# Gate and val products of a gated feed-forward block in seven half-size products instead of eight

## The chip, the cores and the metric

One core of a Trainium2 chip runs the whole program: TensorE (PE) multiplies, VectorE (DVE), ScalarE (ACT) and GpSimd (POOL) do the elementwise work, and transfers are issued on the queue of SyncE (SP). The metric is the device time of one execution in microseconds, as the median of three runs.

## The reference, cut to what matters

Attention over 4 batches of 8 heads gives x with 2304 tokens of 512 features. Two feed-forward blocks follow; the change is in the second, in which gate and val are two products of the same x.

```python
def _moe_ref(x, w_in, w_out, s, b):          # d_ff = 2048
    r = np.maximum(x @ w_in, 0.0)
    return ((s * (r * r) + b) @ w_out)

def _moe2_ref(x, w_gate, w_val, w_out):      # d_ff = 1536
    g = x @ w_gate
    silu = g * (1.0 / (1.0 + np.exp(-g)))
    val = x @ w_val
    return (silu * val @ w_out)
```

The weights arrive as 64-bit floats, the activations as 32-bit ones.

## The kernel before, in words

Every operand of a product is split into a high and a low part (fp32r), and a product is three matmuls: high by high, high by low, low by high (`mm3`). The program has three stages: attention, the first block (`block_b`, five blocks of 512, 512, 512, 384 and 384 tokens) and the second block (`block_2`, the same five blocks of tokens).

In `block_b` a chunk is 128 of the 2048 hidden features. PE makes `hb` (12 matmuls), ACT and DVE make the square and its two parts (`relu`, `sq`, `gh`, `gl`), and PE adds the chunk before it into `acc` (12 matmuls). The normalised x of a block is prepared by `x_load`: a sum of two loads and a product with `rbx`, on POOL, then the split on ACT and DVE.

In `block_2` before the change, for each of the 12 chunks `f`, gate and val take four steps over the 512 features each, three matmuls a step, as wide as the block of tokens (512 or 384 columns). ACT makes silu, DVE multiplies, both split the result, and `second` multiplies it with `out2` (matmuls of 512 columns, 3 for each 128 tokens). All 36 weights stay on chip once they are split.

A weight comes by `weight`: a load of 512 KB into `raw` (3 buffers), four steps that turn it into 32 bits (`d0` on ACT, `d1` to `d3` on DVE, in one of 2 `dec` buffers), then its high part on ACT and its low part on DVE or POOL, in one of 36 weight slots (pools `wa` 10, `wb` 22, `wc` 4), of which the first block's weights take 32.

The order of the instructions is set at build time by `Schedule`: it keeps a clock with assumed durations, and on each engine issues the ready operation of lowest `prio` whose buffers are free. On the chip every engine then works through its own list strictly in that order, and an instruction that waits holds up everything behind it on its engine.

Of the kernel before, what the change touches and what calls it, by code (L numbers as in the profile page):

```python
# [177 lines left out]
def tile_attention_moe_moe(  # L178
# [79 lines left out]
    y_d = [dram.tile([DM, n], F32, name=f"y_d{j}") for j, n in enumerate(UBS)]  # L258
# [13 lines left out]
    W, W_op, W_tok = {}, {}, {}  # L272

    def weight(key, pools, prio, dep=None, hi_eng="act", lo_eng="pool", after=()):
# [7 lines left out]
        raw_tok, slot_tok = Token("raw"), Token(*pools)  # L282
# [11 lines left out]
        o = sch.dma(n * 262144, load, prio, (dep,), (raw_tok,), after=after, pace=1.5)  # L294
# [28 lines left out]
        else:  # L323
            end = (raw_tok,)

        def hi():
            p = wa_p if slot_tok.pool == "wa" else late[slot_tok.pool]
            W[key] = p.tile([128, 2, 512], F32R, tag="w", name="w")
            val = st["val"] if wide else st["raw"]
            if hi_eng == "act":  # L330
                nc.scalar.activation(out=W[key][:, 0], in_=val, func=AF.Copy)  # L331
            else:
                nc.vector.tensor_copy(W[key][:, 0], val)

        def lo():
            val = st["val"] if wide else st["raw"]
            e = nc.gpsimd if lo_eng == "pool" else nc.vector
            e.tensor_tensor(out=W[key][:, 1], in0=val, in1=W[key][:, 0].bitcast(F32), op=ALU.subtract)  # L338
# [400 lines left out]
    def x_load(st, pieces, n, prio, deps, pool_name, pool, batches=None):  # L739

        xh_tok = Token(*pool_name)
# [175 lines left out]
    def block_b(i, j):  # L917
# [8 lines left out]
        outs, xh_tok = x_load(st, pieces, UB, prio - 800 if i else LATE - 900, deps, ("xhb", "xhc"), lambda: late[st["xh_tok"].pool], batches)  # L926
# [12 lines left out]
        for d in range(KD):  # L939
# [5 lines left out]
            y_op[j].append(sch.dma(512 * UB, lambda d=d, st=st, j=j: nc.sync.dma_start(out=y_d[j][d * 128:(d + 1) * 128, :], in_=st["y", d]),  # L945
# [5 lines left out]
    z = 0  # L951
    for f in range(F2):
        for kind in ("gate", "val", "out2"):
            weight((kind, f), ("wb", "wa", "wc"), LATE + 2500 + 120 * z, sw, lo_eng="pool" if z % 2 else "dve")
            z += 1

    def block_2(i, j):
        st = {}
        UB = UBS[j]
        prio = LAST + 2000 * i  # L960
        outs, xh_tok = x_load(st, [(0, UB, (y_d[j],))], UB, prio - 1500 if i else LATE + 1000 * n_b, y_op[j], ("xhb", "xhc"), lambda: late[st["xh_tok"].pool])
        nt = UB // 128
        a_toks = (Token("s"), Token("s"))
        acc_toks = (a_toks[0], a_toks[0], a_toks[1], a_toks[1])
        step = 0
        pend = None
        hs, order = chains["gb"]

        def second(pend, first, last):
            f, gops, g_tok = pend  # L970
            res = []
            for c in range(nt):
                def fn(c=c):
                    if first and c == 0:
                        st["acc"] = []
                        for _ in range(2):
                            t = ps_s.tile([128, 1024], F32, tag="s", name="acc2")
                            st["acc"] += [t[:, 0:512], t[:, 512:1024]]
                    w = W["out2", f]
                    uh, ul = st["u", f]  # L980
                    cs = slice(c * 128, (c + 1) * 128)
                    o = st["acc"][c]
                    nc.tensor.matmul(o, uh[:, cs], w[:, 0], start=first, stop=False)  # L983
                    nc.tensor.matmul(o, uh[:, cs], w[:, 1], start=False, stop=False)  # L984
                    nc.tensor.matmul(o, ul[:, cs], w[:, 0], start=False, stop=last)  # L985
                res.append(op("pe", t_mm(512, 3), fn, prio + step, (*gops, W_op["out2", f], *order[-1:]), a_toks if first and c == 0 else (),
                              (g_tok, W_tok["out2", f])))
                order.append(res[-1])
            return res

        for f in range(F2):
            toks = {}
            last_mm = {}
            for kind in ("gate", "val"):
                tok = toks[kind] = Token("t", "v")
                for kk in range(KD):
                    def fn(kk=kk, f=f, kind=kind, tok=tok):
                        if kk == 0:
                            st[kind, f] = get_hb(tok, UB)
                        w = W[kind, f]  # L1000
                        cs = slice(kk * 128, (kk + 1) * 128)
                        mm3(st[kind, f], w[:, 0, cs], w[:, 1, cs], st["xh"][:, kk], st["xl"][:, kk], kk == 0, kk == KD - 1)
                    hs.append(op("pe", t_mm(UB, 3), fn, prio + step, (outs[kk], W_op[kind, f], *hs[-1:]), (tok,) if kk == 0 else (),
                                 (xh_tok, W_tok[kind, f])))
                    step += 1
                last_mm[kind] = hs[-1]
            r_tok, g_tok = Token("rb2"), Token("gb")
            def silu(f=f):
                st["u", f] = tuple(late["gb"].tile([128, 512], F32R, tag=tag, name=tag)[:, 0:UB] for tag in ("gh", "gl"))
                st["si", f] = late["rb2"].tile([128, 512], F32, tag="r", name="si")[:, 0:UB]  # L1010
                nc.scalar.activation(out=st["si", f], in_=st["gate", f], func=AF.Silu)  # L1011
            def mul(f=f):
                nc.vector.tensor_tensor(out=st["si", f], in0=st["val", f], in1=st["si", f], op=ALU.mult)  # L1013
            def uh(f=f):
                nc.scalar.activation(out=st["u", f][0], in_=st["si", f], func=AF.Copy)  # L1015
            def ul(f=f):
                nc.vector.tensor_tensor(out=st["u", f][1], in0=st["si", f], in1=st["u", f][0].bitcast(F32), op=ALU.subtract)
            o = op("act", t_act(UB), silu, prio + step, (last_mm["gate"],), (r_tok, g_tok), (toks["gate"],))
            o = op("dve", t_dve(UB), mul, prio + step, (o, last_mm["val"]), (), (toks["val"],))
            o1 = op("act", t_act(UB, False), uh, prio + step, (o,))  # L1020
            o2 = op("dve", t_dve(UB), ul, prio + step, (o1,), (), (r_tok,), port=True)
            if pend is not None:
                second(pend, pend[0] == 0, False)
                step += nt
            pend = (f, (o1, o2), g_tok)
        fin = second(pend, False, True)
        for c in range(nt):
            y_tok = Token("rb2")
            def ev(y_tok=y_tok, c=c):
                st["y", c] = late["rb2"].tile([128, 512], F32, tag="r", name="o")  # L1030
                if c % 2:
                    nc.vector.tensor_copy(st["y", c], st["acc"][c])
                else:
                    nc.scalar.activation(out=st["y", c], in_=st["acc"][c], func=AF.Copy)
            o = op("dve" if c % 2 else "act", 0.6, ev, prio + 1900, (fin[c],), (y_tok,), (acc_toks[c],))
            for z in range(2):
                b, g = divmod((sum(UBS[:j]) + c * 128) // 64 + z, PC)
                last = i == len(blocks) - 1 and z == 1
                def put(c=c, z=z, b=b, g=g, e=nc.scalar if last else nc.sync):
                    e.dma_start(out=out[b * S:(b + 1) * S].rearrange("(r g) m -> r g m", g=PC)[:, g], in_=st["y", c][64 * z:64 * z + 64])  # L1040
                sch.dma(131072, put, prio + 1900, (o,), (), (y_tok,), eng="act" if last else "sp")

    for i, j in enumerate(blocks):
        block_2(i, j)
# [45 lines left out]
```

## Time and profile before

| what | value |
|---|---|
| median of 3 runs | 1173.27 us (1172.63 to 1173.53) |
| the profiled execution | 1175.48 us, its span 1173.7 us |
| PE busy | 1143.1 us (97%), 6242 matmuls |
| PE weight loads busy | 1009.1 us (86%) |
| DVE busy | 616.2 us (52%) |
| ACT busy | 551.5 us (47%) |
| POOL busy | 263.6 us (22%) |
| moved by DMA | 110.39 MB, mean 94 GB/s |

Busy is the time that an engine spent on instructions; a matmul's end is modelled and overlaps the next one's start, so how fast matmuls follow each other is read from their starts. In the timeline, times are from the span's start.

### The profile page before, as it was taken

Reading aid. Unit: us, or ns where it says so; the run is one execution under the profiler, and the core shown is the slowest. Engines: PE = TensorE matmul, PEld = TensorE weight load, DVE = VectorE, ACT = ScalarE, POOL = GpSimd, SP = SyncE. Lnnn points to the kernel's source line nnn. Section 1 sums busy time; section 2 is a strip of 40 time slices with the busy share of each in tenths; the row PEclk is TensorE's granted clock in tenths of the full one; section 3 lists DMA queues with packets and bytes.
Section 4 is the critical chain, followed back from the end, with each engine's and each line's share of the span. In section 5 each row is a group of like instructions: output and inputs, shape, how many; then the busy total and the mean of one; then the engine's idle time right before and its main releaser. Section 6 shows DMA issues by size and latency. Waiting matters only on the chain.

```text
span 1173.7 us, 16604 instructions
## 1 busy us (share of the span) xinstructions
PE 1143.1 (97%) x6242; PEld 1009.1 (86%) x6242; DVE 616.2 (52%) x969; ACT 551.5 (47%) x1112; POOL 263.6 (22%) x222
## 2 busy tenths in 40 slices
PE   8989899999999999999999999999999999999998
PEld 7889888898887888888899998888888888899997
DVE  5879788999979943232242798811211211211111
ACT  4879888899877832232232566412111211211211
POOL 6776685743222031020020112200000000000000
PEclk8899999999999999999999999999999999999999
DMA  4588888767375640110110446301100200200100
GB/s 112 117 191 189 228 208 190 201 158 183 94 226 177 216 149 17 56 57 5 64 49 6 135 146 218 112 1 47 25 1 1 63 1 1 63 1 1 27 1 27
DMA packets 126335, 110.39 MB, mean 94 GB/s; under 512 B 68256, under 2 KB 103216, under 8 KB 126256
## 3 DMA queue, kind: packets, MB, share of 16 engines
q1 hardware_dynamic: 126016, 108.95, 34.3%
q8 instruction: 49, 0.80, 0.3%
q10 hardware_dynamic: 240, 0.39, 0.1%
q14 instruction: 30, 0.25, 0.1%
HBM read 69.71 MB, written 18.95 MB: 76 GB/s over the span
## 4 chain that ended last, share of the span: by engine, by line
PE 79%; DVE 8%; ACT 4%; DMA 3%; SPq 2%; issue 2%; POOL 1%; ACTq 0%; POOLq 0%; DVEq 0%
PE hb L798 14%; PE hb L800 14%; PE hb L799 14%; PE acc L799 5%; PE acc L800 5%; PE acc L798 5%; PE acc L983 4%; PE acc L985 4%; PE acc L984 4%; PE ps_s L609 3%; PE ps_t L670 2%; DVE nm L612 2%; SPq L537 2%; DVE pl L685 2%; PE ps_av L700 1%
## 5 line engine op out<-in xcount | busy, mean ns | idle before, releaser
L798 PE MATMUL hb<-xh,w 128*128 128x512 f32 (+1 forms) x800 | 296.3, 370 | 1.9 <-ACT w L331 1.4
L800 PE MATMUL hb<-xh,w 128*128 128x512 f32 (+1 forms) x800 | 296.0, 370 | 0.0
L799 PE MATMUL hb<-xl,w 128*128 128x512 f32 (+1 forms) x800 | 295.6, 370 | 0.0
L1013 DVE TENSOR_TENSOR si<-hb,si 128x512 f32<-128x512 f32 (+1 forms) x60 | 38.3, 638 | 276.4 <-PE hb L800 273.3
L798 PEld LDWEIGHTS hb<-xh,w 128*128 128x128 f32 x800 | 150.2, 188 | 23.8 <-ACT w L331 1.8
L800 PEld LDWEIGHTS hb<-xh,w 128*128 128x128 f32 x800 | 150.1, 188 | 21.0 <-DVE w L338 0.4
L799 PEld LDWEIGHTS hb<-xl,w 128*128 128x128 f32 x800 | 150.1, 188 | 21.0
L799 PE MATMUL acc<-gl,w 128*128 128x512 f32 (+1 forms) x320 | 118.2, 369 | 0.1
L1011 ACT ACTIVATE si<-hb 128x512 f32<-128x512 f32 (+1 forms) x60 | 33.3, 555 | 180.0 <-PE hb L800 174.3
L798 PE MATMUL acc<-gh,w 128*128 128x512 f32 (+1 forms) x320 | 117.9, 368 | 0.0
L800 PE MATMUL acc<-gh,w 128*128 128x512 f32 (+1 forms) x320 | 117.7, 368 | 0.0
L612 DVE TENSOR_REDUCE nm<-ps_s 128x1 f32<-128x576 f32 x144 | 108.3, 752 | 11.7 <-PE ps_s L609 10.4
L609 PE MATMUL ps_s<-t,a 128*128 128x288 f32 x320 | 103.6, 339 | 9.1 <-ACT e L616 7.4
L616 ACT ACTIVATE e<-ps_s,nm 128x576 f32<-128x576 f32 x144 | 107.1, 744 | 8.3 <-DVE nm L612 7.5
L678 ACT ACTIVATE ph<-ps_t 128x512 fp32r<-128x512 f32 x192 | 105.8, 570 | 9.6 <-PE ps_t L670 7.8
L1015 ACT ACTIVATE gh<-si 128x512 fp32r<-128x512 f32 (+1 forms) x60 | 35.4, 589 | 146.2 <-DVE si L1013 146.2
L850 DVE SCALAR_TENSOR_TENSOR r<-r,sv 128x512 f32<-128x512 f32 (+1 forms) x64 | 46.2, 722 | 108.0 <-ACT r L844 108.0
L700 PE MATMUL ps_av<-ph,vh 128*128 128x384 f32 (+1 forms) x320 | 97.8, 326 | 0.4 <-ACT xr L713 0.4
L844 ACT ACTIVATE r<-hb 128x512 f32<-128x512 f32 (+1 forms) x80 | 44.0, 551 | 114.9 <-PE hb L800 103.6
L685 DVE TENSOR_TENSOR pl<-ps_t,ph 128x512 fp32r<-128x512 f32 x144 | 96.0, 684 | 1.8 <-ACT ph L678 0.6
L670 PE MATMUL ps_t<-ident,e 128*128 128x128 f32 x576 | 88.4, 281 | 6.9 <-DVE qklo L515 4.3
L609 PE MATMUL ps_s<-kz,a 128*128 128x288 f32 x320 | 92.8, 305 | 0.1
(80 smaller groups left out, 1962.4 us busy)
## 6 DMA issues: line engine op xcount, KB each, us to landing
raw<-in_moe_w_out_dram SPq DMA_DIRECT2D x28, 512.0 KB, 3.6
x_d<-xr SPq DMA_DIRECT2D x64, 144.0 KB, 2.6
raw<-in_moe_w_in_dram SPq DMA_DIRECT2D x16, 512.0 KB, 3.9
raw<-in_moe_w_gate_dram SPq DMA_DIRECT2D x12, 512.0 KB, 3.5
raw<-in_moe_w_val_dram SPq DMA_DIRECT2D x12, 512.0 KB, 3.7
x<-in_q_dram SPq DMA_DIRECT2D x15, 288.0 KB, 3.6
x<-in_k_dram SPq DMA_DIRECT2D x15, 288.0 KB, 5.0
out_dram<-o SPq DMA_DIRECT2D x33, 128.0 KB, 2.4
```

Source lines behind the costliest of these rows:

```text
L609: nc.tensor.matmul(ps[:, hf * 512:hf * 512 + HS], a[:, q0:q0 + 128], m[:, k0:k0 + HS], start=y == 0, stop=y == len(todo) - 1)
L612: nc.vector.tensor_reduce(out=st["nm"][:, u:u + 1], in_=st["s", u], axis=AX.XY, op=ALU.max, negate=True)
L616: nc.scalar.activation(out=st["e", u].rearrange("p (f n) -> p f n", f=2), in_=st["s", u], func=AF.Exp, bias=st["nm"][:, u:u + 1], accum_ou ...
L670: nc.tensor.transpose(ps[:, z * 128:z * 128 + 128], st["e", u][:, kc * 128:kc * 128 + 128], ident)
L678: nc.scalar.activation(out=st["ph", y][0:rows, 512 * i:512 * i + n], in_=st["pt", y, i][0:rows, 0:n], func=AF.Copy)
L685: nc.vector.tensor_tensor(out=dst, in0=st["pt", y, i][0:rows, 0:n], in1=st["ph", y][0:rows, c].bitcast(F32), op=ALU.subtract)
L700: nc.tensor.matmul(ps, vv, st["ph", y][:, c], start=kc == 0, stop=kc == 4)
L798: nc.tensor.matmul(o, lh, rh, start=first, stop=False)
L799: nc.tensor.matmul(o, lh, rl, start=False, stop=False)
L800: nc.tensor.matmul(o, ll, rh, start=False, stop=last)
L983: nc.tensor.matmul(o, uh[:, cs], w[:, 0], start=first, stop=False)
L984: nc.tensor.matmul(o, uh[:, cs], w[:, 1], start=False, stop=False)
```

## The change

Gate and val of one chunk are now made for 768 tokens at a time (three blocks instead of five). The 512 features are halved, the 768 tokens are halved (`QN` = 384), and gate and val are the two halves of the third direction. By Strassen's scheme (in Winograd's form) seven products of 256 features by 384 tokens, each of 6 matmuls of 384 columns, take the place of eight.

- **Sums of weights.** `combine` loads and decodes gate and val of a chunk, makes four sums on DVE, splits the results into four pairs of parts and stores them (`keep`) in DRAM (`wd`), with the split `out2` as the fifth. This is done four chunks at a time during blocks 1 to 3 of `block_b`. Slots are given back when the store has landed.
- **Sums of x.** `x_load_2` loads four quarters of a block's x and makes four differences (768 columns, DVE) and seven splits (ACT and DVE).
- **A chunk.** `unit` makes the seven products; of their results ACT copies one and DVE adds seven times (384 columns), in buffers of `rb2`, `raw` and `dec`. The first 384 tokens go on to `out2` (`out_proj` with h=0) one chunk later, between the products. For the second 384 tokens the result is kept in six weight slots; after the twelfth chunk these are split and multiplied in one run (`out_proj` with h=1, 12 times 9 matmuls).
- **Stream.** For every block the four parts of each chunk are loaded again from `wd` into weight slots; the 12 parts of `out2` are loaded once and stay.
- In `x_load` the sum and the product with `rbx` of blocks 1 to 4 move from POOL to DVE, and POOL's low parts of weights go to DVE.

```diff
-    y_d = [dram.tile([DM, n], F32, name=f"y_d{j}") for j, n in enumerate(UBS)]
+    y_d = dram.tile([DM, NT], F32, name="y_d")
+    wd = [[dram.tile([2, 128, 512], F32, name=f"wd{f}_{z}") for z in range(5)] for f in range(F2)]
...
+    def keep(f, z, prio, after, dep, n, tok, tile):
+        def put():
+            nc.sync.dma_start(out=wd[f][z].rearrange("h p m -> p h m")[:, :, 0:n], in_=tile()[:, :, 0:n].bitcast(F32))
+        wd_op[f, z] = sch.dma(1024 * n, put, prio, (dep,), (), (tok,), after=after, pace=1.2)
...
+        gst, g_o, g_end = fetch(("gate", f), prio, None, after, (s_tok,))
+        vst, v_o, v_end = fetch(("val", f), prio + 1, None, (W_ld["gate", f],))
...
+        for fn in (s1, s2, s3, s4):
+            o = (op("dve", t_dve(HALF), fn, prio + 2, o, port=True),)
...
+        weight(("out2", f), ALL, prio + 10, None, lo_eng="dve", after=(W_ld["val", f],))
+        keep(f, 4, prio + 10, (), W_op["out2", f], 512, W_tok["out2", f], lambda f=f: W["out2", f])
...
-        for kind in ("gate", "val", "out2"):
-            weight((kind, f), ("wb", "wa", "wc"), LATE + 2500 + 120 * z, sw, lo_eng="pool" if z % 2 else "dve")
+        gate = chains["gb"][0][KD * (F1 * (1 + f // 4) + 3 * (f % 4) + 1)]
+        ld_last = (combine(f, LATE + 1000 * (1 + f // 4) + 700 + 20 * (f % 4), (*ld_last, gate)),)
...
+    PRODS = ((0, 0), (0, 1), (1, 0), (2, 0), (3, 0), (1, 1), (2, 1))
+    X_OF = ("b11", "b21", "t2", "t3", "t4", "t1", "b22")
...
+                    for kk in range(2):
+                        mm3(ps[z], wh, wl, xh, xl, kk == 0, kk == 1)
...
+            for z, when in enumerate((0, 1, 2, 3, 4, 11, 13)):
+                product(z, when)
```

Three places show how the order changes. Names: `r` and `gl` belong to a chunk of the first block, `dec` to decoding, `sums` and `w` to the new sums of weights, `xsum`, `xl`, `xh` to the sums of x.

DVE in block 3 of `block_b`, before:

```order
L850 SCALAR_TENSOR_TENSOR r<-r,sv 128x384 [waits Activation_49]
L862 SCALAR_TENSOR_TENSOR gl<-r,bv,gh 128x384 [waits Activation_49]
L787 TENSOR_TENSOR xl<-xs,xh 128x384 [waits DMAHW2_49,DMAHW1_49,Activation_49]
L850 SCALAR_TENSOR_TENSOR r<-r,sv 128x384 [waits DMAHW5_49,DMAHW0_49,Activation_49]
L862 SCALAR_TENSOR_TENSOR gl<-r,bv,gh 128x384 [waits PE_49,Activation_49]
```

The same engine and block now:

```order
L310 SCALAR_TENSOR_TENSOR dec<-raw,dec 128x512 [waits DMAHW6_49,DVE_49]
L315 SCALAR_TENSOR_TENSOR dec<-raw,dec 128x512 [waits DVE_49]
L874 SCALAR_TENSOR_TENSOR gl<-r,bv,gh 128x384 [waits PE_49,Activation_49]
L993 TENSOR_TENSOR sums<-dec 128x256 [waits DVE_49]
L996 TENSOR_TENSOR sums<-sums,dec 128x256 [waits DVE_49]
L999 TENSOR_TENSOR sums<-dec 128x256
L862 SCALAR_TENSOR_TENSOR r<-r,sv 128x384 [waits Activation_49]
L1002 TENSOR_TENSOR sums<-dec,sums 128x256 [waits DVE_49]
L793 TENSOR_TENSOR xs<-xs,rbx 128x192 [waits DMAHW4_49,DMAHW3_49]
L1021 TENSOR_TENSOR w<-dec,w 128x512
```

The chunk's own `r` and `gl` now stand among decodings, sums, splits and products with `rbx` that wait for transfers. Counted in the whole list, the first sum of the twelve chunks stands after 3, 7, 10 and 14 of a block's sixteen `r` in block 1, after 3, 7, 11 and 14 in block 2, after 4, 9 and 14 in block 3, and the twelfth at the start of block 4.

SP where the second block's loads begin, now (before, all weights were loaded once and only x was loaded for each block):

```order
L1083 DMA xsum<-y_d 128x2x384
L1083 DMA xl<-y_d 128x2x384
L1083 DMA w<-y_d 128x2x384
L1135 DMA w<-wd_4_143 128x2x512
L1142 DMA w<-wd_0_139 128x2x512
L1142 DMA w<-wd_1_140 128x2x512
L1142 DMA w<-wd_2_141 128x2x512
L1142 DMA w<-wd_3_142 128x2x256
L1135 DMA w<-wd_4_148 128x2x512
```

`wd_4` is `out2`, `wd_0` to `wd_3` are the four parts of a chunk; in the list the loads stand four chunks ahead of the last `y_d` stores of the first block.

DVE where block 0 of the second stage ends and block 1 begins, now:

```order
L1242 TENSOR_TENSOR tmp<-hb,tmp 128x384 [waits DVE_49,PE_49]
L1093 TENSOR_TENSOR xsum<-xsum,xl 128x768 [waits DMAHW7_49,DMAHW6_49]
L1278 TENSOR_TENSOR w<-tmp 128x384 [waits Activation_49]
L1302 TENSOR_TENSOR gl<-w,gh 128x384 [waits PE_49]
L1189 COPY o<-acc_8538 128x512 [waits DVE_49,Activation_49]
L1093 TENSOR_TENSOR xsum<-w,xsum 128x768 [waits DMAHW0_49]
L1302 TENSOR_TENSOR gl<-w,gh 128x384 [waits PE_49,Activation_49]
L1093 TENSOR_TENSOR xsum<-w,xsum 128x768
L1104 TENSOR_TENSOR xl<-xl,xh 128x768
```

The first difference of the next block's x, which waits for its loads, stands ahead of the low part (`L1302`) that the run of h=1 matmuls needs. On PE a chunk stands as five products, three matmuls of `out_proj`, a product, three, a product, three; the first two products of the next block are drawn into the run of h=1.

## Rows read from the trace of the kernel before

**Rows 1.** Busy time by stretch, in us (x instructions); last: granted clock, DMA share, GB/s.

```profile
330.00:400.00 70.00, 68.54 (x297) 55.27 (x298) 63.08 (x99) 55.70 (x95) 14.14 (x12) 1.00 0.63 195
400.00:655.00 255.00, 254.98 (x1210) 221.21 (x1209) 93.49 (x132) 84.62 (x143) 34.26 (x38) 1.00 0.21 65
655.00:720.00 65.00, 65.00 (x374) 64.63 (x373) 60.01 (x99) 40.67 (x75) 13.59 (x9) 1.00 0.48 157
...
760.00:1018.00 258.00, 258.00 (x1123) 210.34 (x1122) 50.80 (x77) 45.91 (x78) 1.28 (x1) 1.00 0.07 19
```

**Rows 2.** Waits of PE from 330 us on: us in total, times, longest.

```profile
PE hb L798 <- ACT w L331: 1.4, 1, 1.4
PE hb L798 <- ACT si L1011: 0.6, 1, 0.6
```

**Rows 3.** Timeline of PE, second stage: start us, us, instruction, idle before it.

```profile
716.37 0.39 PE L798 MATMUL hb<-xh,w 128*128 128x512 f32 x1
...
719.82 0.39 PE L798 MATMUL hb<-xh,w 128*128 128x512 f32 x1
...
726.39 0.39 PE L800 MATMUL hb<-xh,w 128*128 128x512 f32 x1
727.36 0.50 PE L798 MATMUL hb<-xh,w 128*128 128x512 f32 x1 [0.57 <-ACT si L1011]
...
1017.78 0.34 PE L798 MATMUL hb<-xh,w 128*128 128x384 f32 x1
...
1168.00 0.39 PE L985 MATMUL acc<-w,gl 128*128 128x512 f32 x1
```

**Rows 4.** Timeline of PE and its weight loads in attention, matmuls of 192 columns.

```profile
300.46 0.28 PE L700 MATMUL ps_av<-ph,vh 128*128 128x192 f32 x1
300.48 0.19 PEld L702 LDWEIGHTS ps_av<-pl,vh 128*128 128x128 f32 x1
...
300.57 0.27 PE L702 MATMUL ps_av<-pl,vh 128*128 128x192 f32 x1
```

**Rows 5.** Busy time by stretch: fullest DMA, and matmuls of 384 columns.

```profile
320.00:325.00 5.00, 5.00 (x24) 4.14 (x23) 0.86 (x3) 3.42 (x7) 1.36 (x1) 1.00 1.01 354
...
600.00:700.00 100.00, 100.00 (x578) 99.87 (x577) 61.01 (x100) 47.49 (x87) 14.34 (x14) 1.00 0.27 84
```

**Rows 6.** Timeline of DVE in block 4 of the first block, without gaps.

```profile
667.64 0.68 DVE L308 SCALAR_TENSOR_TENSOR dec<-raw,dec 128x512 uint32<-128x512 uint32 x1
668.24 0.68 DVE L338 TENSOR_TENSOR w<-dec,w 128x512 fp32r<-128x512 f32 x1
...
669.44 0.60 DVE L862 SCALAR_TENSOR_TENSOR gl<-r,bv,gh 128x384 fp32r<-128x384 f32 x1
669.97 0.60 DVE L850 SCALAR_TENSOR_TENSOR r<-r,sv 128x384 f32<-128x384 f32 x1
```

**Rows 7.** Timeline of DVE, one decoding, each step on the one before.

```profile
330.35 0.42 DVE L305 TENSOR_SCALAR dec<-dec 128x512 uint32<-128x512 uint32 x1
330.81 0.69 DVE L308 SCALAR_TENSOR_TENSOR dec<-raw,dec 128x512 uint32<-128x512 uint32 x1
331.53 0.69 DVE L313 SCALAR_TENSOR_TENSOR dec<-raw,dec 128x512 uint32<-128x512 uint32 x1
```

**Rows 8.** Groups by line and shape: busy us, mean ns of one, idle before.

```profile
L1013 DVE TENSOR_TENSOR si<-hb,si 128x384 f32<-128x384 f32 x24 | 13.4, 557 | 99.4 <-PE hb L800 96.3 <-ACT si L1011 3.1
L1011 ACT ACTIVATE si<-hb 128x384 f32<-128x384 f32 x24 | 11.8, 492 | 64.8 <-PE hb L800 61.8 <-DMA out_dram<-o 3.0
L302 ACT ACTIVATE dec<-raw 128x512 f32<-128x512 f32 x68 | 45.7, 672 | 21.9 <-DVE w L338 10.2 <-POOL w L338 6.7 <-DMA raw<-in_moe_w_in_dram 2.4
```

**Rows 9.** DMA issues: KB each, median us from issue to landing.

```profile
raw<-in_moe_w_gate_dram SPq DMA_DIRECT2D x12, 512.0 KB, 3.5
...
y_d<-y SPq DMA_DIRECT2D x12, 256.0 KB, 3.1
...
xl<-y_d SPq DMA_DIRECT2D x2, 768.0 KB, 4.5
```

More of the change, by code (lines that the diff above doesn't have):

```diff
@@ L270, in dma, with fetch @@
         return sch.dma(size, lambda: nc.sync.dma_start(out=o, in_=i), prio, after=after)
[L272 to L274 removed]
+    W, W_op, W_tok, W_ld = {}, {}, {}, {}
+    def fetch(key, prio, dep=None, after=(), acq=()):
         kind, f = key
@@ L292, in load @@
                 )
-        o = sch.dma(n * 262144, load, prio, (dep,), (raw_tok,), after=after, pace=1.5)
+        o = W_ld[key] = sch.dma(n * 262144, load, prio, (dep,), (raw_tok, *acq), after=after, pace=1.5)
         if wide:
@@ L323, in weight, with value @@
         else:
+            st["val"] = None
             end = (raw_tok,)
+        return st, o, end
+    def weight(key, pools, prio, dep=None, hi_eng="act", lo_eng="pool", after=()):
+        st, o, end = fetch(key, prio, dep, after)
+        slot_tok = Token(*pools)
+        def value():
+            return st["raw"] if st.get("val") is None else st["val"]
         def hi():
@@ L328, in hi @@
             W[key] = p.tile([128, 2, 512], F32R, tag="w", name="w")
-            val = st["val"] if wide else st["raw"]
+            val = value()
             if hi_eng == "act":
@@ L335, in lo @@
         def lo():
-            val = st["val"] if wide else st["raw"]
+            val = value()
             e = nc.gpsimd if lo_eng == "pool" else nc.vector
@@ L949, in tile_attention_moe_moe @@
         block_b(i, j)
-    z = 0
-    for f in range(F2):
-        for kind in ("gate", "val", "out2"):
-            weight((kind, f), ("wb", "wa", "wc"), LATE + 2500 + 120 * z, sw, lo_eng="pool" if z % 2 else "dve")
-            z += 1
-    def block_2(i, j):
-        st = {}
-        UB = UBS[j]
-        prio = LAST + 2000 * i
-        outs, xh_tok = x_load(st, [(0, UB, (y_d[j],))], UB, prio - 1500 if i else LATE + 1000 * n_b, y_op[j], ("xhb", "xhc"), lambda: late[st["xh_tok"].pool])
-        nt = UB // 128
-        a_toks = (Token("s"), Token("s"))
[L964 to L970, printed above, removed]
+    ALL = ("wb", "wa", "wc")
@@ L973, in fn @@
                 def fn(c=c):
[L974 to L980, printed above, removed]
+                    if f == 0 and c == 0 and h == 0:
+                        get()
+                    w = o_st[f]
@@ L981, in fn @@
+                    uh, ul = st["u", h, f]
                     cs = slice(c * 128, (c + 1) * 128)
-                    o = st["acc"][c]
-                    nc.tensor.matmul(o, uh[:, cs], w[:, 0], start=first, stop=False)
+                    o = st["bank"][c if h == 0 else (c + 3) % 4]
+                    nc.tensor.matmul(o, uh[:, cs], w[:, 0], start=f == 0, stop=False)
                     nc.tensor.matmul(o, uh[:, cs], w[:, 1], start=False, stop=False)
-                    nc.tensor.matmul(o, ul[:, cs], w[:, 0], start=False, stop=last)
@@ L1026, in block_2 @@
[L1026 to L1041, printed above, removed]
@@ L1043, in tile_attention_moe_moe, with finish, ev, put @@
-    for i, j in enumerate(blocks):
-        block_2(i, j)
+                    nc.tensor.matmul(o, ul[:, cs], w[:, 0], start=False, stop=f == F2 - 1)
+                res.append(op("pe", t_mm(512, 3), fn, pr + 2 * c, (*gops, o_ld[f], *need(c), *o_order[-1:]), a_toks if f == 0 and c == 0 and h == 0 else (),
+                              (g_tok, o_toks[f])))
+                o_order.append(res[-1])
+            return res
+        def finish(h, fin, pr, last):
+            for c in range(nt):
+                y_tok = Token("rb2")
+                def ev(c=c):
+                    st["y", h, c] = late["rb2"].tile([128, 512], F32, tag="r", name="o")
+                    a = st["bank"][c if h == 0 else (c + 3) % 4]
+                    if c % 2:
+                        nc.vector.tensor_copy(st["y", h, c], a)
+                    else:
+                        nc.scalar.activation(out=st["y", h, c], in_=a, func=AF.Copy)
+                o = evs[c] = op("dve" if c % 2 else "act", 0.6, ev, pr, (fin[c],), (y_tok,), a_toks if h else ())
+                for z in range(2):
+                    b, g = divmod((2 * QN * i + QN * h + c * 128) // 64 + z, PC)
+                    other = last and z == 1
+                    def put(c=c, z=z, b=b, g=g, e=nc.scalar if other else nc.sync):
+                        e.dma_start(out=out[b * S:(b + 1) * S].rearrange("(r g) m -> r g m", g=PC)[:, g], in_=st["y", h, c][64 * z:64 * z + 64])
+                    sch.dma(131072, put, pr, (o,), (), (y_tok,), eng="act" if other else "sp")
@@ L1046, in tile_attention_moe_moe @@
+        finish(1, fin, prio + 60 * F2 + 200, last)
+    for i in range(NT // (2 * QN)):
+        block_2(i)
     with tc.manual_schedule():
```

284 lines of the change are left out of this document (240 added, 44 removed).

## The prediction

> **What bounds the kernel now.** I read the busy times by stretch first. From 400 us to the end of the matmuls PE has work without a gap: 254.98 of 255 us, 65.00 of 65, 258.00 of 258 [rows 1]. The list of PE's waits confirms it: after 330 us PE waited twice, 1.4 and 0.6 us [rows 2]. So the time of the second stage is a number of matmuls times the distance between their starts, and only what changes that number, that distance, or makes PE wait, counts. The other engines are far from full in most of it (DVE 50.80 of 258 us from 760 on), but not everywhere: from 655 to 720, where the second stage's weights are decoded, DVE worked 60.01 of 65 us and PE still did not wait; from 330 to 400, where the first block's weights are decoded beside the first chunks, DVE worked 63.08 of 70 and PE lost 70 - 68.54 = 1.46 us [rows 1].
>
> The timeline of PE gives the distances [rows 3]. The three blocks of 512 tokens have 3 x 432 = 1296 matmuls of 512 columns; six of them stand early, at 716.37, so 1290 lie between 719.82 and 1017.78. One gap, 727.36 - 726.39 less an ordinary 0.23, is a stall of 0.74. (297.96 - 0.74) / 1290 = 0.2304 us each. The two blocks of 384 run from 1017.78 to 1168.23 (the last start and one distance): 150.45 us for 216 matmuls of 512 columns (49.8 us) and 576 of 384, so 100.7 / 576 = 0.1748 us for 384 columns. The stage took 297.96 + 150.45 + 6 x 0.2304 = 449.8 us.
>
> **The change, part by part.**
>
> *Matmuls.* Removed: 1440 for gate and val (864 of 512 columns, 576 of 384). Added: 3 blocks x 12 chunks x 42 = 1512 of 384 columns. The `out2` matmuls stay 648. New stage without waits: 1512 x 0.1748 + 648 x 0.2304 = 264.3 + 149.3 = 413.6 us. Gain 449.8 - 413.6 = **36.2 us**. At the distance of the stretch from 600 to 700 us, 100 / 578 = 0.173 [rows 5], it would be 39: that is its upper end.
>
> A narrower matmul pays off only while the weight load in front of it does not set the distance. From 600 to 700 us, at 384 columns, weight loads were busy 99.87 of 100 us [rows 5]. But in attention matmuls of 192 columns, each with a weight load of 0.19 us of its own, start 300.57 - 300.46 = 0.11 us apart [rows 4], so loads overlap and 384 columns are not bound by them. The Trainium skill, page "Perfetto Trace Analysis", section "Identifying the Most-Contended Engine", holds that the busy share of LDWEIGHTS, not of matmuls, is a good measure of how near TensorE is to its limit. By that rule the 384-column stretch is already at the limit of loading and this change adds loads; rows 4 speak against that reading.
>
> *A chunk of the second stage.* PE needs 42 x 0.1748 + 9 x 0.2304 = 9.4 us (and 2.1 later, for h=1). DVE has ten operations of 384 columns (seven sums, two products, one low part) at 0.557 [rows 8]: 5.6 us; ACT four at about 0.49: 2.0. Both fit. Nor does PE run out of PSUM: there are four banks, the first result is copied within a microsecond of its product, and each sum ends before the product after next (1.05 us a product against 0.56 a sum). The low part for `out_proj` is needed five products later, over 5 us. I cost this at nothing; the cover is DVE's 3.8 us a chunk.
>
> *The stream.* A chunk's four parts are 1792 KB, 1.835 MB in 9.4 us: 195 GB/s; in the first block of tokens with `out2` 2.36 MB, 251 GB/s. The trace holds 354 GB/s with the DMA engines full [rows 5]. At the start four chunks lie ready (20 of 36 slots are neither x nor kept results), later two to three. On SP four loads take about 2.4 us a chunk to issue. Cost zero; its bound is under the rivals.
>
> *Sums of weights, in blocks 1 to 3 of the first block.* DVE gets per chunk of weights three decodings, four sums and five low parts: 3 x (0.4 + 0.6 + 0.6) + 4 x 0.33 + 4 x 0.6 + 0.33 = 8.9 us at the distances of back-to-back operations [rows 6]. Its place is 3.67 chunks of 24 matmuls, 3.67 x 24 x 0.226 = 19.9 us in blocks 1 and 2 (0.173 and 128 columns more at 2.4 GHz, an estimate) and 4.67 x 24 x 0.173 = 19.4 in block 3. With `r` and `gl` (0.53 at 384 columns [rows 6], about 0.66 at 512) and x now on DVE (7 us a block), that is 15 to 16 of 19.9 us: 80%, below the 92% of 655 to 720 at which PE did not wait. But the twelve are one chain: 3 `raw` and 2 `dec` buffers allow hardly more than one at a time. Along it: two loads (issue 0.6 each, 3.5 to land [rows 9]) 4.7, ACT 0.7 [rows 8], two decodings, 1.77 each when every step waits for the last (0.46 + 0.72 + 0.6 [rows 7]) 3.5, four sums on each other 1.7, the first split 1.2, `out2`'s decoding 2.5, signals 1: 15.3, and 4 to 5 us of the running chunks' operations in between. It just fits 19.9. Since the order is fixed, each microsecond over is paid by PE, twelve times. The store of 512 KB is not in the trace; bounds: below, the 256 KB store's 3.1 us; above, the 768 KB load's 4.5 [rows 9]; I take 3.7, nearer the store. Measured loss in comparable stretches: 0 in 65 us (655 to 720) and 1.46 in 70 (330 to 400). For some 236 us that is 0 to 4.9; I take **2.5**, the middle.
>
> *Borders of the second stage.* Before its second and third block, x (1.5 MB) is loaded, landing some 4.5 us [rows 9] plus 768 KB at 354 GB/s = 2.2 after its issue, and DVE makes 11 operations of 768 columns (about 0.9 each, 1.5 times the 0.60 of 512 [rows 6]): 10 us, among the low parts that the h=1 run needs. Against 24.9 us of that run (108 x 0.2304) this is hidden, but the first difference stands ahead of the first low part and waits for transfers. From 0 (loads land before) to 3 us (loads start only when the last product is over) a border; I take 1.5: **3** for two. The first block's x is prepared 25 us ahead, beside the first block's last chunks: zero.
>
> *The rest.* The 0.74 us stall is already in the 449.8; ACT's table load now falls into a chunk whose result is not needed for 5 us. The end (last copies and stores) is as before. POOL loses work that nobody waited for.
>
> **Sum.** -36.2 + 2.5 + 3 = -30.7 us. The profiled execution took 1175.48 (span 1173.7 and 1.8 around it), giving 1144.8; it lies 2.2 above the median of 1173.27, so the median becomes **1142.6**, told as 1143. Likeliest, with 0 to 39 us bounds on its terms: 1134 to 1150; chance 0.72.
>
> **The rivals.**
>
> 1. *The chain of the weight sums paces the first block, on the losing side.* Mechanism as above: DVE and ACT wait in a fixed order for a load, a store that frees a slot or a buffer, and `r` and `gl` of the running chunk queue behind. For it: rows 1 show a loss where decoding and chunks share DVE, five stores of an unseen size pass four free slots, and all 12 stand in one line. Against: 655 to 720. It decides at 33 / 12 = 2.8 us beyond its place for each of the twelve; at 4 us it gives -36.2 + 48 + 3 = +15: 1188. Chance 0.07. In between (1 to 2 us each, 12 to 24 us): 1152 to 1164, chance 0.12.
> 2. *The stream sets the pace.* The gain is gone when a chunk takes 33 / 36 = 0.9 us longer, that is, if the stream gives 1.835 / 10.3 = 178 GB/s instead of 195. For it: from 655 to 720 DMA moved only 157 GB/s. Against: it did so at a share of 0.48, with the loads waiting for buffers [rows 1]. At 157, a chunk takes 11.7 us: 36 x 2.3 = 83 us, 1225. Chance 0.03.
> 3. *Weight loads set the distance of narrow matmuls.* Then 1512 x 0.19 = 287 us instead of 264: gain 13.2 - 5.5 = 8 us, 1165. Against: rows 4. Chance 0.03.
> 4. *No difference.* That the change does not do what it says is excluded by the list: 1512 matmuls of 384 columns stand there for gate and val. The time stays within 2.3 us only where rival 1 takes nearly all of the gain, at 2.8 us for each of the twelve. Chance 0.03.
>
> **How the numbers follow.** About 0.2%, 2.3 us, is what a measurement of this kernel can tell from no change. Faster: 0.72 + 0.12 + 0.03 (rival 3) + 0.01 (a mild rival 2) = 0.88; same 0.03; slower 0.07 + 0.02 = 0.09. The range reaches from 1134 (all losses zero, and the shorter distance) to 1160 (half of rival 1's middle).
>
> **What would show it.** Right: in the second stage PE busy without gaps, about 414 us from its first product to its last matmul; 1512 matmuls 0.175 apart; DMA share near 0.6 there; DVE at 60%; waits of PE in blocks 1 to 3 of the first block below 5 us, and at each border a microsecond or two behind a low part. Wrong: waits of PE for `gl` in blocks 1 to 3 that recur twelve times (rival 1), waits of a product for a DMA (rival 2), 384-column starts 0.19 apart (rival 3).

## The result, and the profile after

The change takes 1137.14 us (median of 4 runs, 1134.56 to 1137.56), the kernel before in the same comparison 1173.40: a ratio of 0.9683 [0.9662, 0.9703], 36.3 us less. The forecast was 1143, its range 1134 to 1160. Differences of the experiments are given below as differences of such ratios, times 1173.4 us.

The page of the changed kernel, busy times, one group of DVE and the largest groups of transfers:

```profile
span 1132.8 us, 18005 instructions
...
PE 1107.0 (98%) x6314; PEld 1012.0 (89%) x6314; DVE 800.7 (71%) x1394; ACT 593.0 (52%) x1199; POOL 190.5 (17%) x156
...
L1242 DVE TENSOR_TENSOR tmp<-hb,tmp 128x384 f32<-128x384 f32 x252 | 139.8, 556 | 114.5 <-PE hb L812 113.6
...
w<-wd SPq DMA_DIRECT2D x120, 512.0 KB, 4.3
wd<-w SPq DMA_DIRECT2D x48, 512.0 KB, 3.6
```

PE is busy 36 us less with 72 more matmuls; DVE has 184 us more work and waits for PE before its sums (113.6 us). The store of 512 KB, unknown before, lands in 3.6 us (3.7 was taken).

The stretches of the changed kernel (windows; the columns are those of [rows 1]):

```profile
330.00:400.00 70.00, 69.90 (x309) 57.44 (x308) 58.33 (x106) 55.94 (x93) 0.00 (x0) 1.00 0.55 170
400.00:655.00 255.00, 255.00 (x1221) 222.96 (x1220) 191.72 (x357) 126.55 (x222) 0.00 (x0) 1.00 0.66 221
655.00:700.00 45.00, 45.00 (x262) 45.00 (x261) 27.02 (x43) 18.89 (x33) 0.00 (x0) 1.00 0.67 224
...
720.00:850.00 130.00, 128.72 (x673) 119.76 (x672) 77.00 (x137) 36.48 (x68) 0.00 (x0) 1.00 0.62 201
850.00:1000.00 150.00, 149.89 (x786) 139.92 (x785) 87.78 (x157) 41.24 (x77) 0.00 (x0) 1.00 0.57 185
```

Where weight sums are made (400 to 655), DVE works 75% of the time and PE all of it. In the second stage PE has no gap but one, from 720 to 850; DVE stands at 59%, as forecast, DMA at 0.62. PE's list of waits after 330 us has this one entry (waited for: us in total, times, longest):

```profile
PE acc L1174 <- ACT o L1191: 1.3, 1, 1.3
```

For the ledger, PE's timeline, first of the kernel before (the first matmul of its first block), then of the change (that same place, the first and the seventh matmul of the second stage, the gap, the last matmul):

```profile
318.62 0.39 PE L798 MATMUL hb<-xh,w 128*128 128x512 f32 x1
```

```profile
314.34 0.39 PE L810 MATMUL hb<-xh,w 128*128 128x512 f32 x1
...
709.50 0.34 PE L810 MATMUL hb<-xh,w 128*128 128x384 f32 x1
...
712.62 0.34 PE L810 MATMUL hb<-xh,w 128*128 128x384 f32 x1
...
824.33 0.39 PE L1176 MATMUL acc<-w,gl 128*128 128x512 f32 x1
826.00 0.50 PE L1174 MATMUL acc<-w,gh 128*128 128x512 f32 x1 [1.28 <-ACT o L1191]
...
1126.83 0.39 PE L1176 MATMUL acc<-w,gl 128*128 128x512 f32 x1
```

In both kernels six matmuls of the second stage stand early; they are counted there. With one more distance behind the last start, the two profiled executions divide so:

| stretch | before | after | difference | forecast |
|---|---|---|---|---|
| attention, to the first `hb` | 318.6 | 314.3 | -4.3 | 0 |
| first block | 399.8 | 397.2 | -2.6 | +2.5 |
| second block | 449.8 | 415.5 | -34.3 | -36.2 + 3 |
| behind the last matmul | 5.5 | 5.7 | +0.2 | 0 |
| span | 1173.7 | 1132.8 | -40.9 | -30.7 |

The first row is no effect of the change, which leaves attention as it is: over the 13 profiles of this case, the first `hb` came between 313.94 and 319.00 us, without order in which kernel it was. The other rows sum to -36.7, which fits the 36.3 of the medians. So two things are to be explained: the 34.3 of the second stage, and a first block that became shorter with twelve chains of new work in it. In the experiments the first stage is taken from the first `hb` to the first `hb<-w` of the second stage (399.3 us in the change), the second from there to the last matmul's start (413.2).

**Theory A.** PE is the bound from the first `hb` on. The second stage gains by the number of its matmuls alone. The first block gained because POOL lost its work: before, DVE's operations were held up beside POOL's, and what waited for them cost PE a few microseconds. **Rivals:** the chain of weight sums, the stream, and weight loads, as in the prediction; and, for the first block, that its 2.6 us are scatter. Where an expectation names Theory A this is meant, and B is the rival at which the run is aimed.

### The profile page after: what moved, and what is told of

Read it like the earlier page. It is cut to its first block, busy times and chain, and to the rows that moved or that the text cites. A ratio compares the mean times of both kernels' runs of the same rounds, so it can differ in the third digit from the quotient of the medians.

```text
span 1132.8 us, 18005 instructions
## 1 busy us (share of the span) xinstructions
PE 1107.0 (98%) x6314; PEld 1012.0 (89%) x6314; DVE 800.7 (71%) x1394; ACT 593.0 (52%) x1199; POOL 190.5 (17%) x156
## 5 line engine op out<-in xcount | busy, mean ns | idle before, releaser
L1242 DVE TENSOR_TENSOR tmp<-hb,tmp 128x384 f32<-128x384 f32 x252 | 139.8, 556 | 114.5 <-PE hb L812 113.6
L812 PE MATMUL hb<-xh,w 128*128 128x384 f32 (+1 forms) x560 | 199.1, 356 | 0.0
L810 PE MATMUL hb<-xh,w 128*128 128x384 f32 (+1 forms) x560 | 199.0, 355 | 0.0
L811 PE MATMUL hb<-xl,w 128*128 128x384 f32 (+1 forms) x560 | 198.9, 355 | 0.0
L811 PEld LDWEIGHTS hb<-xl,w 128*128 128x128 f32 x560 | 105.2, 188 | 10.4
L810 PEld LDWEIGHTS hb<-xh,w 128*128 128x128 f32 x560 | 105.3, 188 | 10.3
L812 PEld LDWEIGHTS hb<-xh,w 128*128 128x128 f32 x560 | 105.2, 188 | 8.0
L1257 ACT ACTIVATE tmp<-tmp 128x384 f32<-128x384 f32 x72 | 37.7, 524 | 111.2 <-DVE tmp L1242 108.9
L811 PE MATMUL hb<-w 128*128 128x384 f32 x264 | 89.0, 337 | 0.0
L812 PE MATMUL hb<-w 128*128 128x384 f32 x264 | 89.0, 337 | 0.0
L810 PE MATMUL hb<-w 128*128 128x384 f32 x264 | 88.6, 336 | 0.0
```

Source lines behind the costliest of these rows:

```text
L810: nc.tensor.matmul(o, lh, rh, start=first, stop=False)
L811: nc.tensor.matmul(o, lh, rl, start=False, stop=False)
L812: nc.tensor.matmul(o, ll, rh, start=False, stop=last)
L1242: nc.vector.tensor_tensor(out=st[dst, f], in0=ps[z], in1=st[a, f], op=ALU.add)
```

## The experiments

**eight: the count of products.** In the change, the seventh product is made twice over, so it enters its sum doubled.

```diff
-                    for kk in range(2):
+                    for r, kk in [(r, kk) for r in range(2 if z == 6 else 1) for kk in range(2)]:
```

> The changed kernel with the seventh product of each chunk made twice (its result is doubled, so this output is not the reference's): 36 x 6 = 216 more matmuls of 384 columns, nothing else, in the same order on every engine. Theory A (the gain is the number of matmuls, all else is hidden): 216 x 0.1748 = 37.8 us slower than the change, 1175, that is 0 to 3 us above before. Theory B (waits on DVE, ACT or the stream are already part of the second stage's pace): less than 30 us slower, since the added matmuls fill waits.

Measured: 1175.77 us, ratio 1.0014 [0.9999, 1.0028], 38.8 us above the change; the second stage took 450.6 us, 37.5 more, and PE waited nowhere that it had not before. 216 matmuls at 37.5 / 216 = 0.174 us. The count of matmuls, put back, puts the whole gain back.

**nopool and xpool: POOL's part.** In the kernel before, x's sum and product with `rbx` in blocks 1 to 4, and the low parts of the second stage's weights, move from POOL to DVE, as the change has it; in the change, x goes back to POOL.

```diff
-        outs, xh_tok = x_load(..., batches)
+        outs, xh_tok = x_load(..., batches, "dve" if i else "pool")
...
-            weight((kind, f), ("wb", "wa", "wc"), LATE + 2500 + 120 * z, sw, lo_eng="pool" if z % 2 else "dve")
+            weight((kind, f), ("wb", "wa", "wc"), LATE + 2500 + 120 * z, sw, lo_eng="dve")
```

```diff
-        outs, xh_tok = x_load(..., batches, "dve" if i else "pool")
+        outs, xh_tok = x_load(..., batches, "pool")
```

> The kernel before, with the sum of x and its product with rbx of blocks 1 to 4 on DVE and every low part of the second stage's weights on DVE, as in the change, but with eight products. Theory A (POOL's part of the work was what made the first block 2.6 us longer before: DVE cannot run beside a POOL operation, and PE waited 1.4 us for a weight at 330 to 400 us): 1.5 to 3 us faster than before, and PE busy over 69.8 of 70 us from 330 to 400. Theory B (the 2.6 us are scatter between executions): within 1 us of before.

> The changed kernel, with the sum of x and its product with rbx back on POOL. Theory A: 1.5 to 3 us slower than the change (ratio to before 0.970 to 0.972 against 0.968), with waits of PE in the first block. Theory B: the same as the change within 1 us.

Measured: nopool 1172.34 us, 0.9974 [0.9961, 0.9988], 3.0 us faster than before; xpool 1145.65 us, 0.9754 [0.9738, 0.977], 8.3 us slower than the change, more than expected of it. The stretch from 312 to 400 us (windows) shows the first part of it, in the order before, nopool, xpool and the change:

```profile
312.00:400.00 88.00, 86.18 (x391) 69.62 (x390) 76.07 (x123) 69.20 (x120) 18.55 (x15) 1.00 0.60 187
```

```profile
312.00:400.00 88.00, 87.64 (x398) 71.93 (x397) 76.65 (x139) 71.25 (x122) 3.19 (x3) 1.00 0.64 196
```

```profile
312.00:400.00 88.00, 86.17 (x391) 69.61 (x390) 74.90 (x122) 69.19 (x120) 18.11 (x15) 1.00 0.58 175
```

```profile
312.00:400.00 88.00, 87.65 (x386) 71.70 (x386) 71.07 (x127) 69.39 (x117) 2.98 (x2) 1.00 0.59 182
```

With 18 us of POOL, PE works 86.2 of 88 us; with 3, 87.6. DVE has more operations without POOL (139 instead of 123) and is hardly busier: the operations that were long beside POOL became short. Counted in the timelines of DVE and POOL, from 330 us to the end of the first block: in the kernel before, 28 of the 63 DVE operations that overlap one of POOL's took over 15% longer than the median of their kind, 18.2 us more in sum, and none of the other 264 did. In nopool and in the change POOL does nothing there, and none did.

PE's one long wait of the first block leads back to such an operation (kernel before, timelines of POOL, DVE, ACT and PE). The step of 1.79 us makes ACT late, and ACT's row DVE, which then works without a gap from 359.59 to 364.70; ACT, late again for DVE, works without a gap from 363.58 up to the weight that PE waits for:

```profile
356.66 1.68 POOL L778 TENSOR_TENSOR xs<-xl,xh 128x512 f32<-128x512 f32 x1 [3.62 <-DVE gl L860]
...
357.10 1.79 DVE L313 SCALAR_TENSOR_TENSOR dec<-raw,dec 128x512 uint32<-128x512 uint32 x1
...
358.93 0.63 ACT L331 ACTIVATE w<-dec 128x512 fp32r<-128x512 f32 x1 [1.04 <-DVE dec L313]
...
366.01 0.61 ACT L331 ACTIVATE w<-dec 128x512 fp32r<-128x512 f32 x1
...
366.67 0.50 PE L798 MATMUL hb<-xh,w 128*128 128x512 f32 x1 [1.36 <-ACT w L331]
```

How long an operation is held up is plainest later on (kernel before, timeline, DVE and POOL):

```profile
670.26 1.80 POOL L338 TENSOR_TENSOR w<-dec,w 128x512 fp32r<-128x512 f32 x1 [5.09 <-ACT w L331]
...
670.95 1.67 DVE L308 SCALAR_TENSOR_TENSOR dec<-raw,dec 128x512 uint32<-128x512 uint32 x1
672.54 0.61 DVE L862 SCALAR_TENSOR_TENSOR gl<-r,bv,gh 128x384 fp32r<-128x384 f32 x1
673.07 0.68 DVE L313 SCALAR_TENSOR_TENSOR dec<-raw,dec 128x512 uint32<-128x512 uint32 x1
```

The decoding step that starts while POOL works takes 1.67 us and ends behind POOL's operation (672.06); its twin two rows on takes 0.68. The Trainium skill, page "SBUF — State Buffer", section "SBUF: two separate sides", says that the two engines share one pair of ports as an exclusive lock: GpSimd, or VectorE in a two-port mode or with two inputs from SBUF, whichever starts first, holds it for its whole instruction. The row agrees.

ACT did wait for POOL's own results in the kernel before: from 312 to 720 us 16.0 us for x (`xh` for `xs`) and 5.1 for low parts (`dec` for `w`). But all except 0.2 us of that lies behind 400 us, where PE worked 254.98 of 255 and 65.00 of 65 us [rows 1].

In the change it matters more, since DVE has more to do: xpool's waits of PE are those of the kernel before (1.4 us for `w`, [rows 2]) and five new ones for the first block's `gh` and `gl`, 2.0 us, and its first stage is 5.9 us longer (405.3). Those at 426 and 604 us follow DVE operations of 1.1 to 1.5 us beside POOL; the two at 596 (0.7 us) follow a wait of ACT for the stores of `y`, so not all of the 5.9 is shown to be the lock. The other 2.4 of the 8.3 are within the spread of attention. So the first block's gain comes with POOL's work: from the first `hb` to the matmul that starts 1900 later it is 396.4 us before, 393.8 in nopool and 393.8 in the change. Giving work to another engine also changes the order of the lists, and no run holds that fixed.

**chain1, chain2, chain4: the chain of weight sums.** The four sums of every weight chunk are written one, two or four times more, with the same values: 4, 8 or 16 more dependent operations in each of the twelve chains. Two rounds took 2.93 us on DVE (from 470.55 to 473.48 in one of them).

```diff
+            for _ in range(2):
+                nc.vector.tensor_tensor(out=stage(1), in0=gv(vst, 0), in1=gv(vst, 1), op=ALU.add)
+                nc.vector.tensor_tensor(out=stage(0), in0=stage(1), in1=gv(gst, 0), op=ALU.subtract)
+                nc.vector.tensor_tensor(out=stage(2), in0=gv(gst, 0), in1=gv(vst, 0), op=ALU.subtract)
+                nc.vector.tensor_tensor(out=stage(3), in0=gv(gst, 1), in1=stage(0), op=ALU.subtract)
```

> The changed kernel with the four sums of weights made three times over (the same result), in an unchanged order: each of the twelve chains of weight sums is 8 dependent operations of 256 columns longer, about 0.42 us each, 3.4 us. Rival 1's account (the chain just fits its place, each microsecond over is paid twelve times): up to 41 us slower than the change, 1170 to 1178. The account by slack (each chain has a few microseconds of reserve before a chunk's own operations are late): 0 to 8 us slower.

> The same with the sums made five times over: 16 operations, 6.8 us more a chain. DVE then has 15.7 + 6.8 = 22.5 us of work in 19.9, so at least 12 x 2.6 = 31 us slower than the change by either account; by rival 1's 82 us. The difference between this run and the one with 3.4 us tells where the reserve ends.

> The change, with the four sums of each weight chunk made twice (four more dependent operations of 256 columns, half of what chain2 added: 2.93 / 2 = 1.47 us for each of the twelve chains). Theory A (reserve of 0.3 us a chain, as chain2 and chain4 gave it): the first stage grows by 12 x (1.47 - 0.3) = 14 us. Rival B (the reserve was larger, and chain2's 31 us held a loss of the clock that comes only with long waits): 12 x 1.47 less up to 1.2 each, 3 us or less.

| kernel | us | ratio | against the change | first stage | added, 12 times |
|---|---|---|---|---|---|
| chain1 | 1149.03 | 0.9782 [0.9755, 0.9809] | +11.6 | +11.6 | 1.47 |
| chain2 | 1169.72 | 0.9952 [0.9936, 0.9968] | +31.6 | +31.3 | 2.93 |
| chain4 | 1211.35 | 1.0304 [1.0267, 1.0341] | +72.9 | +70.8 | 5.87 |

The second stage is the same in all three (413.2). Each microsecond added comes out at the end twelve times, but for the first 1.47 - 11.6 / 12 = 0.5 (chain1) or 2.93 - 31.3 / 12 = 0.3 us (chain2); in chain4 nothing is left of it (5.87 - 70.8 / 12 = 0.0). The account by slack (0 to 8 us in chain2) missed. PE's list of waits in chain2, and two rows of its timeline:

```profile
PE acc L811 <- DVE gl L874: 14.2, 13, 3.0
PE acc L810 <- ACT gh L869: 4.6, 5, 1.4
```

```profile
473.48 0.74 DVE L874 SCALAR_TENSOR_TENSOR gl<-r,bv,gh 128x512 fp32r<-128x512 f32 x1
...
474.28 0.50 PE L811 MATMUL acc<-gl,w 128*128 128x512 f32 x1 [2.97 <-DVE gl L874]
```

They are the waits for `gl` and `gh` that rival 1 named, in almost every chain: here `gl` stands right behind the added operations (to 473.48), and PE waits for it as long as they took. So rival 1's mechanism is real and was half a microsecond a chain from costing time; it cost the change nothing that can be seen. The half microsecond is the reserve behind the sums in DVE's list. Whether the whole chain, loads and stores included, is as near to its place isn't shown: no run lengthens it elsewhere.

**stream15, stream20: the stream.** While the second stage streams its parts, two (stream15) or all four (stream20) of a chunk's parts are also copied from DRAM to DRAM, into tensors that nothing reads.

```diff
+                    if z in (0, 1, 2, 3):
+                        nc.sync.dma_start(out=junk[i][f][z].rearrange("h p m -> p h m")[:, :, 0:n], in_=wd[f][z].rearrange("h p m -> p h m")[:, :, 0:n])
```

> The changed kernel; beside two of each chunk's four loads the same 512 KB are also copied from DRAM to unused DRAM: 2.88 MB in 9.4 us, 307 GB/s, in place of 195. If the stream has reserve up to the 354 GB/s of the fullest stretch: 0 to 5 us slower than the change. If it is already near its limit: 20 us or more slower, with waits of products for loads.

> The same beside all four loads: 3.67 MB in 9.4 us, 390 GB/s, more than the fullest stretch showed. At 354 GB/s the first block of tokens needs 50 MB / 354 = 142 us for 112 us of chunks, the others 124 of 136: 10 to 30 us slower than the change, most of it in the first block of tokens. Under 5 us would mean that a copy inside DRAM costs less than its bytes.

Measured: 1140.69 us, 0.9698 [0.9661, 0.9735], which can't be told from the change, and 1142.00, 0.9713 [0.9683, 0.9742], 3.5 us above it, 2.1 of them in the second stage; the 10 to 30 us expected of stream20 missed. The windows of stream20:

```profile
710.00:1000.00 290.00, 287.38 (x1503) 267.37 (x1502) 166.66 (x295) 80.82 (x150) 0.00 (x0) 1.00 0.95 347
```

At 347 GB/s and a share of 0.95, PE still works 287.4 of 290 us; its new waits (0.9, 0.4, 0.4) are for sums and parts, none for a load of `wd`, though these land 7.4 us after their issue instead of 4.3 (medians of the 512 KB loads). With the change alone it is 185 to 201 GB/s there, so the stream is far from being the bound, and rival 2 falls.

**banks: the gap at the border.** In the 1.28 us gap (826.00 above) PE waits for ACT's copy of a finished sum, in a pair of PSUM banks of which it needs the other one; on ACT a split of x (0.83 us) stands ahead of that copy (the change, timeline of ACT):

```profile
824.14 0.60 ACT L1191 ACTIVATE o<-acc 128x512 f32<-128x512 f32 x1 [0.68 <-PE acc L1176]
824.63 0.83 ACT L1102 ACTIVATE xh<-xl 128x768 fp32r<-128x768 f32 x1
825.36 0.59 ACT L1191 ACTIVATE o<-acc 128x512 f32<-128x512 f32 x1
```

The kernel of this run takes the banks of the second run in another order, so that the first needed is in the pair whose copies are done.

```diff
-                    o = st["bank"][c if h == 0 else (c + 3) % 4]
+                    o = st["bank"][((2, 0, 1), (3, 2, 0))[h][c]]
...
-                    a = st["bank"][c if h == 0 else (c + 3) % 4]
+                    a = st["bank"][((2, 0, 1), (3, 2, 0))[h][c]]
```

> The changed kernel, with the PSUM banks of out_proj in another order, so that the first matmuls of the h=1 run write beside the bank that is copied out first, not beside the one that is copied last. Theory A (the 1.3 us wait of PE at the first border is for the last copy in the same two-bank tile): that wait goes, 1.3 us faster than the change, ratio 0.967. Theory B (PE waits there for the low part behind the first difference of x in any case): a wait of 0.5 to 1.3 us stays, now for DVE.

Measured: 1138.39 us, 0.9691 [0.9673, 0.9709], not to be told from the change; the gap is gone and the second stage 412.0 us, 1.1 less. So the border cost what its row shows, and a microsecond is below what the runs resolve.

**low6, low11: DVE's cover in the second stage.** The prediction costed DVE's new work in a chunk at nothing, with a cover of 3.8 us. Here the low part of a chunk's result is written 6 or 11 times, with the same values.

```diff
             def lowp():
-                nc.vector.tensor_tensor(out=st["u", 0, f][1], in0=st["m", f], in1=st["u", 0, f][0].bitcast(F32), op=ALU.subtract)
+                for _ in range(6):
+                    nc.vector.tensor_tensor(out=st["u", 0, f][1], in0=st["m", f], in1=st["u", 0, f][0].bitcast(F32), op=ALU.subtract)
```

> The change, with the low part of each chunk of the second stage's first run written six times over (same values): five more operations of 384 columns on DVE, 5 x 0.557 = 2.8 us a chunk, 36 chunks, 100 us of DVE in all. Theory A (DVE has a cover of 3.8 us in a chunk of 9.4, and the four PSUM banks carry PE over a pause of 3 us): 0 to 3 us more than the change, no recurring wait of PE. Rival B (DVE's place in the order matters and not its share; the sums behind the low part are then late for PSUM): PE waits for a bank in each chunk, 0.5 to 2 us x 36 = 18 to 70 us more.

> The same low part written eleven times: ten more operations, 5.6 us a chunk, so DVE has 11.2 us of work in a chunk of 9.4. Theory A: DVE becomes the bound, 1.8 us a chunk over, 36 x 1.8 = 64 us more than the change, with DVE near 100% in the second stage up to each h=1 run, which gives none of it back; PE waits for banks. If the cover were larger than 5.6 us: nothing.

Measured: low6 1188.91 us, 1.012 [1.0094, 1.0146], 51 us above the change; low11 1365.74, 1.1621 [1.1592, 1.1651], 227 above it. Both missed what Theory A expected; its rival B was right. DVE's timeline shows why, first a chunk of the change, then one of low6:

```profile
782.55 0.56 DVE L1242 TENSOR_TENSOR tmp<-hb,tmp 128x384 f32<-128x384 f32 x1 [0.54 <-PE hb L812]
783.03 0.55 DVE L1268 TENSOR_TENSOR gl<-tmp,gh 128x384 fp32r<-128x384 f32 x1
783.49 0.55 DVE L1242 TENSOR_TENSOR tmp<-hb,tmp 128x384 f32<-128x384 f32 x1
784.32 0.56 DVE L1242 TENSOR_TENSOR tmp<-hb,tmp 128x384 f32<-128x384 f32 x1 [0.27 <-PE hb L812]
785.46 0.56 DVE L1278 TENSOR_TENSOR w<-tmp 128x384 f32<-128x384 f32 x1 [0.59 <-ACT tmp L1257]
787.15 0.56 DVE L1242 TENSOR_TENSOR tmp<-hb,tmp 128x384 f32<-128x384 f32 x1 [1.13 <-PE hb L812]
...
794.88 0.56 DVE L1278 TENSOR_TENSOR w<-tmp 128x384 f32<-128x384 f32 x1 [0.59 <-ACT tmp L1257]
```

```profile
780.49 0.56 DVE L1279 TENSOR_TENSOR w<-tmp 128x384 f32<-128x384 f32 x1 [0.59 <-ACT tmp L1257]
...
786.20 3.51 DVE L1269 TENSOR_TENSOR gl<-tmp,gh 128x384 fp32r<-128x384 f32 x6
789.63 1.01 DVE L1242 TENSOR_TENSOR tmp<-hb,tmp 128x384 f32<-128x384 f32 x2
791.23 0.56 DVE L1279 TENSOR_TENSOR w<-tmp 128x384 f32<-128x384 f32 x1 [0.59 <-ACT tmp L1257]
```

The free time of a chunk lies in pieces of 0.3 to 1.1 us between the sums, each of which waits for its product. The low part stands right before the last sums, and these give back the PSUM banks that PE needs for the next chunk's products. 3.51 - 0.55 = 2.96 us more at this place make the chunk 791.23 - 780.49 = 10.74 us long instead of 794.88 - 785.46 = 9.42: PE pays 1.32, so the cover here is 2.96 - 1.32 = 1.6 us, not 3.8. PE's waits in low6 come once in each of 36 chunks:

```profile
PE hb L810 <- DVE tmp L1242: 34.7, 36, 1.1
```

In low11 DVE's place grows by 6.48 - 0.55 = 5.93 us, of which 1.6 are covered: 4.3 a chunk, and PE's waits are 4.0 us each. DVE, expected near 100%, works only 206.75 of 300 us from 800 to 1100. But the second stage lost 642.6 - 413.2 = 229.4 us, 6.4 a chunk. The other 2.1 are told of in the last section.

## Why the prediction was right, and where not

**Matmuls: right.** Without the gap, the second stage took 415.5 - 1.3 = 414.2 us, and 413.6 was forecast. The distance at 384 columns did not grow where loads are dense: 655 to 700 us has 262 matmuls in 45.00 us, 0.172 each, with weight loads busy 45.00. The Trainium skill, page "Perfetto Trace Analysis", section "Identifying the Most-Contended Engine", judges TensorE's headroom by LDWEIGHTS busy share (and by MFU, its share of peak arithmetic), which would put this stretch at its limit. Here the measurement decides: with 1512 such matmuls in the second stage, and 216 more in eight, the distance stayed at 0.174, not 0.19, and rival 3 (1165 us) falls.

**Sums of weights in the first block, +2.5, and POOL at nothing: the step that failed, in sign.** I took the loss from two stretches of before, 0 and 1.46 us, and spread it over 236 us. But the 1.46 went when POOL's work went: nopool's PE works 69.90 of 70 us from 330 to 400. Nopool and the change take the same 393.8 us over those 1900 matmuls, so the twelve chains cost nothing instead of 2.5, and the work that leaves POOL, which had no term, gave 2.6 back: -2.6 instead of +2.5. The sentence "POOL loses work that nobody waited for" was the mistake. ACT waited for it, as [rows 8] already show (6.7 us behind POOL's `w`), though not where PE lost time; what counted were DVE's operations beside it, up to three times as long, and ACT and PE waited for those. Of the 6.2 us by which the three terms together were high, this is 5.1; the borders are 1.7, the matmuls -0.6.

**"It just fits 19.9": right, by luck as much as by the sum.** 15.3 + 4 to 5 us against 19.9 left 0 to 0.6; the runs found 0.3 to 0.5 behind the sums. The point at which rival 1 was to take the gain away, 2.8 us a chain, is confirmed: chain2 adds 2.93 and is left with 0.9952. The length of the chain itself was not measured, so the agreement of the two numbers shows little; whether it cost anything hung on the last half microsecond, finer than the sum could tell.

**Borders, 3: 1.3.** One border cost 1.3; at the other one matmul started 0.27 late, which stands with the matmuls here. Not the transfers but a copy on ACT, with a split of x ahead of it, made PE wait; a low part, which the prediction had named, was not the cause.

**Chunks at no cost: right in the result, wrong in the reason.** "The cover is DVE's 3.8 us a chunk" is a share of time. What counts is how late the sum that frees a bank may be, and that is 1.6 us.

**Stream at no cost: right**, with a reserve beyond what I had to assume (347 GB/s borne, copies counted, 195 needed).

## What to carry to other kernels

Where an engine is full and nothing makes it wait, count its instructions and multiply by their distance; that part of the forecast held to a microsecond in 400. The idle share of a helper engine is no cover: find in its ordered list the operation that gives something back, and measure how much may stand ahead of it (3.8 us idle in a chunk were worth 1.6). When work leaves an engine, look at what ran long beside it, not only at who waited for it.

## What was not expected of the hardware

After the waits of 4 us in low11 PE comes back at half speed. PE's timeline and the windows of low11, around one of its waits:

```profile
803.29 0.69 PE L810 MATMUL hb<-xh,w 128*128 128x384 f32 x1 [4.01 <-DVE tmp L1242]
```

```profile
800.00:802.00 2.00, 0.00 (x0) 0.00 (x0) 1.90 (x4) 0.00 (x0) 0.00 (x0) 1.00 0.53 192
...
804.00:806.00 2.00, 2.00 (x7) 2.00 (x7) 0.89 (x2) 0.63 (x2) 0.00 (x0) 0.50 0.00 0
806.00:808.00 2.00, 2.00 (x8) 2.00 (x8) 0.69 (x2) 0.53 (x1) 0.00 (x0) 0.50 0.38 131
808.00:810.00 2.00, 2.00 (x9) 2.00 (x8) 0.64 (x2) 0.00 (x0) 0.00 (x0) 0.65 0.00 0
810.00:812.00 2.00, 2.00 (x12) 1.86 (x12) 1.13 (x3) 0.20 (x1) 0.00 (x0) 1.00 0.15 25
```

The granted clock is 0.50 (1.2 GHz) when PE resumes, with some 8 instead of 12 matmuls in 2 us, and 1.00 again from 810 on. From 803.29 to 809.48 the timeline has 19 distances of 384 columns, 6.19 us instead of 19 x 0.174 = 3.3: 2.9 us are lost behind this wait. Summed over the second stage, the starts that come late otherwise than at a wait cost 83 us: 1.4 to 3.0 behind each of the 36 waits, 2.3 in the mean. That accounts for the 2.1 a chunk that the waits leave open. In low6, with waits of 1.0 us as often, the granted clock from 720 to 1180 is 1.00. In chain2 and chain4, with longest waits of 3.0 and 4.6 us, it is 0.99 and 0.93 from 400 to 655. So the sum of the waits doesn't give their price: low6's 36 waits of 1 us cost 50 us, low11's 36 of 4 us 230.
